# Score rests ahead of the values, and first scores in the small tiles' banks: one change to a fused attention and expert kernel

## The chip, the cores and the metric

The kernel runs on one NeuronCore of a Trainium2 chip. The metric is device microseconds (us) of one execution, by the median of several runs. The core has a matrix engine (TensorE, called PE in the profile; its weight loads are shown apart as PEld), VectorE (DVE), ScalarE (ACT), GpSimd (POOL) and SyncE (SP, which here only issues DMAs). Each takes its own queue of instructions in order, and they wait for each other through semaphores. PE writes into PSUM, which has eight banks; a tile of 128 x 448 float32 takes one.

## What is computed

The reference chains three parts. Attention over 4 batches of 12 heads (448 tokens, 64 numbers a head) with a sigmoid in place of the softmax; a gated product; and a soft mixture of 8 experts with 4 slots each:

```python
scores = scale * np.matmul(q, k.transpose(0, 1, 3, 2)) - np.log(S)
attn = 1.0 / (1.0 + np.exp(-scores))
x = np.matmul(attn, v)
...
x = (x @ w_a) * (x @ w_b) @ w_out
...
logits = x @ phi
d = softmax of logits over the tokens
slot_input = d.T @ x
h = np.maximum(slot_input[e] @ w1[e], 0.0)
slot_out[e] = h @ w2[e]
c = softmax of logits over the slots
return c @ slot_out
```

## The kernel before

**Pairs and groups.** Attention works on pairs of heads, numbered g = 0 to 23 (six pairs a batch). Keys and queries are split into a high and a low part (`kh`, `kl`, `qh`, `ql`), and a block of scores is the sum of three matmuls per head, each 64 numbers deep, the two heads side by side on the upper and the lower half of PE's rows (`emit_S`, line 230). ScalarE turns each block into weights `a` with a sigmoid (`sigmoid`, line 247, instruction at 249). The values are matmuls of `a` with `v` (`emit_PV`, line 268; lines 273, 279, 286), and their result is copied out in `emit_x` (line 303).

**Pairs from 14 on** (`GQ` = 14) are laid out otherwise than those ahead of them. Their 448 keys are cut into three blocks of 128 (first, second and third scores, c = 0, 1, 2) and a rest of 64. The rests of two neighbouring pairs, so of a group of four heads, are put together into two full blocks: `emit_S_rest` (line 252), called at the odd pair, does both pairs' rests with four matmuls of 64 x 64 (line 258). They use the whole query and a copy `kr` of the last 64 keys. It then issues, at pairs 15 and 19, the four DMAs of a later query.

**Order.** `att` (line 321) is a generator that writes the instructions in a fixed order; at each `yield` the main loop may put in a step of other work (`fill_step`: group products, logits; and operands of the next stage). A step of `att` for pair g is: split keys and queries of pair g + 1 (`emit_TK`, on VectorE: transpose, high part, low part, for keys and for queries), first scores of pair g (for pair 23 also the second ones; `first`, line 328), values of pair g - 1, second and third scores of pair g, and, at an odd pair, the rest. The main loop leaves `att` at line 1145, once the rest of pair 23 is written; the values of pair 23 come later, between the first products of the next stage (line 843).

**PSUM banks.** While attention runs, the eight banks are shared out by tags: four `sc`, two `ab`, two `ms`. A tile of a tag takes the bank that has been longest in use, and its first matmul waits until the last reader of that bank's former tile is done. `ms()` hands out the small tiles' banks: transposes (line 624, read by a copy at line 626), small transposes of the logits (line 919, read at line 920), the values of pairs 12 and 13 (line 273), the first scores of the odd pairs from 15 on, and the rests. First scores of the even pairs from 14 on, and all second and third scores, take `sc`. `emit_S` picks the tag:

```python
by_ms = c == 0 and (g % 2 if g >= GQ else g >= GT0)
sc = [ms((n, S)) if by_ms and (g >= GQ or not h) else ps_tile("ab" if ab else "sc", [n, S], 2 if ab else 4)
      for h in range(2)]
```

**After attention** come two batches' products in seven parts (line 843), the last batch's products (line 660), and the experts, whose weights stream in by DMA through a ring of buffers (lines 1229 to 1323).

Of the kernel before, what the change touches and what calls it, by code (L numbers as in the profile page):

```python
# [18 lines left out]
B, H, S, D = 4, 12, 448, 64  # L19
DM, FF, NS, NE, F = 768, 1536, 32, 8, 1024  # L20
C = 4
# [5 lines left out]
NP = H // 2  # L27
NE1, NE2 = 17, 4
ST0, ST1, PP, RAWS = 10, 39, (3, 7), (2, 3, 10, 14)
GT0 = 2 * NP + 1  # L30
GQ = 2 * NP + 2
# [9 lines left out]
def body(ctx, tc, q, k, v, w_a, w_b, w_out, phi, w1, w2, out):  # L41
# [19 lines left out]
    def ps_tile(tag, shape, bufs):  # L61
        return psp.tile(shape, F32, tag=tag, name=tag, bufs=bufs)
# [6 lines left out]
    def ms(shape=(128, S)):  # L69
        tags = banks[run["banks"]]  # L70
        tag = tags[run["ms"] % len(tags)]
        run["ms"] += 1
        return ps_tile(tag, list(shape), 4 if tag == "sc" else 2)
# [53 lines left out]
    def chunks_of(g):  # L127
        return (T, C) if g < GQ else (128, 3)
# [71 lines left out]
    def emit_TK(g):  # L200
        if g >= B * NP:
            return
        if g >= GT0:
            for nm in "kq":
                t = transposed(g, nm)
                split_heads(g, nm, t, dve.tensor_copy)
                if g >= GQ:
                    if nm == "k":
                        kr = atp.tile([128, 64], F32, tag="kr", name="kr", bufs=3)
                        act.copy(kr, t[:, 384:])  # L210
                        t = kr
                    whole[nm, g] = t
                if nm == "k" or g not in (GQ + 2, GQ + 6):
                    load_qkv(g + 3, nm)
            return
        tk = transposed(g, "k")
        if not g:
            tq = transposed(g, "q")
        split_heads(g, "k", tk, dve.tensor_copy)
        if not g:  # L220
            split_heads(g, "q", tq, act.copy)

    def emit_TQ(g):
        if g >= B * NP:
            return
        split_heads(g, "q", transposed(g, "q"), dve.tensor_copy)

    a_t = {}

    def emit_S(g, chunks):  # L230

        (kh, kl), (qh, ql) = stk[g]["k"], stk[g]["q"]
        n, _ = chunks_of(g)
        for c in chunks:
            ab = (g < NP or 2 * NP < g < GQ) and c == 2
            by_ms = c == 0 and (g % 2 if g >= GQ else g >= GT0)
            sc = [ms((n, S)) if by_ms and (g >= GQ or not h) else ps_tile("ab" if ab else "sc", [n, S], 2 if ab else 4)
                  for h in range(2)]
            cs = slice(c * n, (c + 1) * n) if g < GQ else slice(c, 384, 3)
            for i, (kx, qx) in enumerate(((kh, qh), (kl, qh), (kh, ql))):  # L240
                for h in range(2):
                    r = slice(64 * h, 64 * h + 64)
                    pe.matmul(sc[h], kx[r, cs], qx[r], start=(i == 0), stop=(i == 2))  # L243
            for h in range(2):
                sigmoid(g, h, c, sc[h], n)

    def sigmoid(g, h, c, sc, n):
        a = atp.tile([128, S], F32, tag="a", name="a", bufs=11)[:n]
        act.activation(a, sc, AF.Sigmoid, bias=nlog[:n], scale=1.0 / math.sqrt(D))  # L249
        a_t[g, h, c] = a  # L250

    def emit_S_rest(g):

        sc = [ms() for _ in range(2)]
        for d in range(2):
            for h in range(2):
                r, f = slice(64 * h, 64 * h + 64), 64 * d
                pe.matmul(sc[h][f:f + 64], whole["k", g - 1 + d][r], whole["q", g - 1 + d][r], start=True, stop=True)
        for h in range(2):
            sigmoid(g, h, 3, sc[h], 128)  # L260
        for d in range(2):
            del whole["k", g - 1 + d], whole["q", g - 1 + d]
        if g in (GQ + 1, GQ + 5):
            load_qkv(g + 4, "q")
# [3 lines left out]
    def emit_PV(g):  # L268
        if g < GQ:
            pv = pv_t[g] = ps_tile("sc", [128, S], 4) if g < 2 * NP else ms()  # L270
            for c in range(C):
                for h in range(2):
                    pe.matmul(pv[64 * h:64 * h + 64], qkv_t["v", g][:, h, c, :], a_t.pop((g, h, c)),  # L273
                              start=(c == 0), stop=(c == C - 1))
            return
        pv = pv_t[g] = ps_tile("ab", [128, S], 2)
        for c in range(3):
            for h in range(2):
                pe.matmul(pv[64 * h:64 * h + 64], qkv_t["v", g][:, h, c], a_t.pop((g, h, c)),  # L279
                          start=(c == 0), stop=False)  # L280
        if g % 2:
            a = [a_t.pop((g, h, 3)) for h in range(2)]
            for d in range(2):
                for h in range(2):
                    s = slice(64 * d, 64 * d + 64)
                    pe.matmul(pv_t[g - 1 + d][64 * h:64 * h + 64], qkv_t["v", g - 1 + d][s, h, 3], a[h][s],  # L286
                              start=False, stop=True)
# [15 lines left out]
    def emit_x(g):  # L303
        pv = pv_t.pop(g)
        qkv_t.pop(("v", g))
        b, kk = divmod(g, NP)
        if b:
            xt[g] = raw_x(b, kk)
            (dve.tensor_copy if g > GQ and g % 2 else act.copy)(xt[g], pv)
        else:  # L310
            xh = x0p.tile([128, S], F32R, tag=f"xh{kk}", name=f"xh{kk}")
            xl = x0p.tile([128, S], F32R, tag=f"xl{kk}", name=f"xl{kk}")
            act.activation(xh, pv, AF.Copy)
            dve.tensor_tensor(xl, pv, xh.bitcast(F32), op=ALU.subtract)
            xt[g] = (xh, xl)
        if g < GQ:
            load_qkv(g + 3, "v")
        if g >= GQ - 1 and g % 2:
            load_qkv(g + 4, "v")

    def att():

        emit_TK(0)
        yield 860
        for g in range(B * NP + 1):
            more = g < B * NP
            dense = g < NP or g >= 2 * NP
            first = ((0, 1) if g in (0, B * NP - 1) else (0,) if dense else ()) if more else ()
            if g:
                emit_TK(g + 1)  # L330
                if g > GQ and g % 2:
                    load_qkv(g + 3, "v")
                yield 430
            for c in first:
                emit_S(g, (c,))
                run["done"] = True
                yield 800
            if g:
                if g < NP and more:
                    emit_TQ(g + 1)  # L340
                    yield 430
                emit_PV(g - 1)
                if g <= GQ:
                    emit_x(g - 1)
                elif g % 2 == 0:
                    emit_x(g - 2)
                    emit_x(g - 1)
                yield 3200
            else:
                emit_TK(g + 1)  # L350
                yield 430
            if not more:
                return
            if not dense:
                emit_S(g, (0, 1))
                yield 1600
                emit_TQ(g + 1)
                yield 430
                emit_S(g, (2, 3))
                yield 1600  # L360
            else:
                if not g:
                    emit_TQ(g + 1)
                    yield 430
                for c in range(chunks_of(g)[1]):
                    if c not in first:
                        emit_S(g, (c,))
                        yield 800
                if g >= GQ and g % 2:
                    emit_S_rest(g)  # L370
                    yield 800

    PAIR = 860 + 4 * 800 + 3200
    att_g = att()
    att_state = [0]

# [193 lines left out]
    def fill_step():  # L570
        while fill:
            if next(fill[0], 0) is None:
                return
            fill.pop(0)
# [561 lines left out]
    for cost in att_g:  # L1136
        if then and then[0][0] in xt:
            then.pop(0)[1]()
        if not run.pop("trans", False):
            fill_step()  # L1140
        run.pop("done", None)
        if next(ops, 0) == 0:
            pu = pu or prep_u(0)
            next(pu, None)
        if (4 * NP - 1, 0, C - 1) in a_t:
            break
    run.pop("exp")()
    for _ in ops:
# [95 lines left out]
    for n in range(0, len(order1), 4):  # L1244
        _, g, x, _ = order1[n]
# [103 lines left out]
```

## Time and profile before

| | |
|---|---|
| runs | 664.79, 665.39, 662.77 us; median 664.79 |
| profiled execution | 664.73 us, of which the span of the program is 662.8 us |
| PE | busy 633.0 us, 96% of the span |
| VectorE, ScalarE, GpSimd | 380.1, 296.6 and 308.4 us |
| DMA | 154.25 MB, mean 233 GB/s |
| first scores of pair 14 | at 219.77 us |
| values of pair 23 begin | at 278.79 us |

The span runs from the first instruction to the last; the profiled execution's own time is that of the same execution as the runs are timed. In timelines a line gives the start, the time from the start of the first to the end of the last instruction merged in it, and, in brackets, how long the engine had been idle before and what ended that. An operand is named output<-inputs. `128*64` is the shape of PE's array that a matmul uses (rows by columns). Ends of matmuls are modelled, so the distance between starts is the safer reading.

### The profile page before, as it was taken

What the parts mean: (1) busy time and instruction counts of PE and PEld (TensorE: products, weight loads), DVE (VectorE), ACT (ScalarE), POOL (GpSimd) and SP (SyncE); (2) the same over time, 40 slices, a digit from 0 to 9 for tenths busy, and PEclk for the clock granted to TensorE, in tenths of its full rate; (3) what the DMA queues carried; (4) which work ended last, traced back from release to release, by engine and by line L of the source; (5) the groups of instructions that cost most, each with busy time, mean ns of one, the idle gap of its engine ahead of it and who ended that gap; (6) DMA issues with size and microseconds to landing.
All of it is one profiled execution on the core that took longest, in us unless ns stands there. A gap on an engine that the chain in (4) does not pass through costs nothing.

```text
span 662.8 us, 10904 instructions
## 1 busy us (share of the span) xinstructions
PE 633.0 (96%) x4015; PEld 449.9 (68%) x4015; DVE 380.1 (57%) x557; ACT 296.6 (45%) x534; POOL 308.4 (47%) x236
## 2 busy tenths in 40 slices
PE   6999999999999999999999999999999998997685
PEld 4557777777776555489988989888879895442121
DVE  4765797788774879588777766744324322200013
ACT  4888889889774677754423322202010002110022
POOL 0233676777644248579976575543334441000000
PEclk9999999999999999999999999999999999998798
DMA  9998999989968676501213423242999999999998
GB/s 204 280 258 221 298 305 291 314 268 300 278 166 184 112 150 143 179 1 47 96 49 103 111 89 101 69 134 80 347 372 333 384 369 344 410 415 416 409 374 303
DMA packets 145396, 154.25 MB, mean 233 GB/s; under 512 B 74336, under 2 KB 121792, under 8 KB 142272
## 3 DMA queue, kind: packets, MB, share of 16 engines
q1 hardware_dynamic: 138768, 150.01, 72.5%
q10 hardware_dynamic: 6576, 3.56, 1.9%
q8 instruction: 32, 0.52, 0.3%
q14 instruction: 20, 0.16, 0.1%
HBM read 126.36 MB, written 27.17 MB: 232 GB/s over the span
## 4 chain that ended last, share of the span: by engine, by line
PE 83%; DMA 11%; ACT 2%; DVE 2%; issue 1%; ACTq 1%; SPq 0%; DVEq 0%
PE ab L660 28%; PE sc L843 16%; DMA e<-in_moe_w 9%; PE sc L243 8%; PE ab L843 8%; PE sc L273 5%; PE ab L279 3%; PE ms L195 2%; PE ms L936 2%; PE ms L581 1%; DMA gkp<-in_moe_w 1%; PE ms L480 1%; PE ms L493 1%; PE ab L243 1%; ACT a L249 1%; PE ab L286 1%
## 5 line engine op out<-in xcount | busy, mean ns | idle before, releaser
L454 POOL TENSOR_TENSOR w<-gk,cy 128x768 int32<-128x768 int32 x36 | 66.2, 1842 | 80.1 <-DVE gk L449 35.3
L249 ACT ACTIVATE a<-sc,sums 112x448 f32<-112x448 f32 (+1 forms) x147 | 83.1, 650 | 15.8 <-PE sc L243 15.7
L660 PE MATMUL ab<-t,wh 128*128 128x448 f32 x288 | 65.1, 371 | 0.0
L660 PEld LDWEIGHTS ab<-t,wh 128*128 128x128 f32 x288 | 53.4, 188 | 6.1 <-issue 1.3
L551 POOL TENSOR_TENSOR wl<-wr,wh 128x768 fp32r<-128x768 f32 x16 | 29.5, 1841 | 49.7 <-DVE wh L550 31.9
L551 POOL TENSOR_TENSOR wl<-w,wh 128x768 fp32r<-128x768 f32 x24 | 45.0, 1878 | 10.1 <-ACT wh L550 10.1
L667 ACT COPY misc<-ab 128x448 f32<-128x448 f32 x24 | 12.7, 531 | 82.1 <-PE ab L660 75.2
L1275 PE MATMUL ab<-e,gk 128*32 128x384 f32 x240 | 34.3, 560 | 9.5 <-DMA e<-in_moe_w 9.5
L670 DVE TENSOR_TENSOR misc<-misc,ab 128x448 f32<-128x448 f32 x24 | 14.8, 616 | 43.9 <-PE ab L660 43.9
L273 PE MATMUL sc<-a,vn 112*64 112x448 f32 x192 | 38.7, 545 | 0.2 <-ACT a L249 0.2
L243 PE MATMUL sc<-qh,kh 64*112 64x448 f32 (+1 forms) x147 | 34.9, 447 | 1.0 <-ACT qh L183 0.6
L723 ACT CAST wx<-T 128x384 fp32r<-128x384 f32 x21 | 10.8, 513 | 55.7 <-DVE T L745 39.1
L660 PE MATMUL ab<-xh,wh 128*128 128x448 f32 x144 | 34.9, 377 | 0.0
L660 PE MATMUL ab<-xl,wh 128*128 128x448 f32 x144 | 34.7, 376 | 0.0
L724 POOL TENSOR_TENSOR wx<-T,wx 128x384 fp32r<-128x384 f32 x23 | 24.6, 1070 | 21.1 <-ACT wx L723 18.0
L660 PE MATMUL ab<-xh,wl 128*128 128x448 f32 x144 | 34.3, 373 | 0.0
L660 PE MATMUL ab<-t,wl 128*128 128x448 f32 x144 | 34.3, 373 | 0.0
L724 POOL TENSOR_TENSOR wx<-wr,wx 128x384 fp32r<-128x384 f32 x29 | 32.4, 1117 | 3.7 <-ACT wx L723 3.6
L1322 DVE COPY o<-sc 128x384 f32<-128x384 f32 x10 | 5.4, 554 | 48.2 <-PE sc L1301 47.0
L447 DVE TENSOR_SCALAR mf<-gk 128x768 f32<-128x768 f32 x24 | 22.7, 947 | 17.2 <-ACT gk L430 17.2
L660 PEld LDWEIGHTS ab<-xl,wh 128*128 128x128 f32 x144 | 25.9, 188 | 9.4 <-issue 7.7
L1275 PEld LDWEIGHTS ab<-e,gk 128*32 128x32 f32 x240 | 9.8, 120 | 32.8 <-DMA e<-in_moe_w 20.7
(492 smaller groups left out, 1526.6 us busy)
## 6 DMA issues: line engine op xcount, KB each, us to landing
e<-in_moe_w SPq DMA_DIRECT2D x23, 1024.0 KB, 8.5
e<-in_moe_w SPq DMA_DIRECT2D x23, 768.0 KB, 15.1
wr<-ab SPq DMA_DIRECT2D x14, 768.0 KB, 4.4
ab<-w SPq DMA_DIRECT2D x24, 384.0 KB, 6.4
gk<-gk SPq DMA_DIRECT2D x24, 224.0 KB, 4.0
e<-in_moe_w SPq DMA_DIRECT2D x14, 384.0 KB, 8.8
wr_cv<-in_moe_w_a SPq DMA_DIRECT2D x6, 768.0 KB, 7.9
wr_all<-in_moe_w_b SPq DMA_DIRECT2D x6, 768.0 KB, 6.8
```

Of the source, the lines that this page charges most:

```text
L243: pe.matmul(sc[h], kx[r, cs], qx[r], start=(i == 0), stop=(i == 2))
L249: act.activation(a, sc, AF.Sigmoid, bias=nlog[:n], scale=1.0 / math.sqrt(D))
L273: pe.matmul(pv[64 * h:64 * h + 64], qkv_t["v", g][:, h, c, :], a_t.pop((g, h, c)), start=(c == 0), stop=(c == C - 1))
L279: pe.matmul(pv[64 * h:64 * h + 64], qkv_t["v", g][:, h, c], a_t.pop((g, h, c)), start=(c == 0), stop=False)
L447: dve.tensor_scalar(mf, m, LOW, HIGH, op0=ALU.max, op1=ALU.min)
L454: pool.tensor_tensor(thirds(w), m.bitcast(I32), thirds(cy_t.pop(x)), op=ALU.add)
L551: pool.tensor_tensor(wl, t, wh.bitcast(F32), op=ALU.subtract)
L660: pe.matmul(t, w[:, kk * 128:(kk + 1) * 128], xt[b * NP + kk][xi], start=(s == 0 and kk == 0), stop=(s == 2 and kk == KD - 1))
L670: dve.tensor_tensor(g, g, t, op=ALU.mult)
L724: pool.tensor_tensor(w[:, 1], t, w[:, 0].bitcast(F32), op=ALU.subtract)
L843: pe.matmul(t, w[:, wi, k * 128:(k + 1) * 128], xs[ORDER[m], k][xi], start=(s == 0 and k == 0), stop=(s == 2 and k == 2))
L1275: pe.matmul(sps[h][32 * j:32 * j + 32], hT[:, 2 * x + i, 2 * j + g], ring[order2[n + j]][0][:, i, c0:c0 + w], start=(g == 0 and x == 0 and ...
```

## The change

First scores of every pair from 13 on are now handed to `ms` (for pairs from 14 on both heads' tiles), the rests take `sc` banks, and the rest of a group is written in the odd pair's step right after its first scores and ahead of the even pair's values. Since the rest of pair 23 is now written earlier, the main loop's end looks for its third scores.

```diff
--- before.py
+++ after.py
@@ -233,7 +233,7 @@
         n, _ = chunks_of(g)
         for c in chunks:
             ab = (g < NP or 2 * NP < g < GQ) and c == 2
-            by_ms = c == 0 and (g % 2 if g >= GQ else g >= GT0)
+            by_ms = c == 0 and g >= GT0
             sc = [ms((n, S)) if by_ms and (g >= GQ or not h) else ps_tile("ab" if ab else "sc", [n, S], 2 if ab else 4)
                   for h in range(2)]
             cs = slice(c * n, (c + 1) * n) if g < GQ else slice(c, 384, 3)
@@ -251,7 +251,7 @@
 
     def emit_S_rest(g):
 
-        sc = [ms() for _ in range(2)]
+        sc = [ps_tile("sc", [128, S], 4) for _ in range(2)]
         for d in range(2):
             for h in range(2):
                 r, f = slice(64 * h, 64 * h + 64), 64 * d
@@ -334,6 +334,9 @@
             for c in first:
                 emit_S(g, (c,))
                 run["done"] = True
+                yield 800
+            if more and g > GQ and g % 2:
+                emit_S_rest(g)
                 yield 800
             if g:
                 if g < NP and more:
@@ -366,9 +369,6 @@
                     if c not in first:
                         emit_S(g, (c,))
                         yield 800
-                if g >= GQ and g % 2:
-                    emit_S_rest(g)
-                    yield 800
 
     PAIR = 860 + 4 * 800 + 3200
     att_g = att()
@@ -1142,7 +1142,7 @@
         if next(ops, 0) == 0:
             pu = pu or prep_u(0)
             next(pu, None)
-        if (4 * NP - 1, 0, C - 1) in a_t:
+        if (4 * NP - 1, 0, C - 2) in a_t:
             break
     run.pop("exp")()
     for _ in ops:
```

How this moves the instructions, at the places that the prediction speaks of. On PE at pair 14 (`ident` is the identity that a transpose multiplies by, `misc` what is transposed, `a` and `vn` weights and values of pair 13, `ls_d` the logits):

```order
 L243 MATMUL sc<-ql,kh 112x448 x2
 L624 MATMUL ms<-ident,misc 128x128 x4
-L243 MATMUL sc<-qh,kh 128x448 x2
-L243 MATMUL sc<-qh,kl 128x448 x2
-L243 MATMUL sc<-ql,kh 128x448 x2
+L243 MATMUL ms<-qh,kh 128x448 x2
+L243 MATMUL ms<-qh,kl 128x448 x2
+L243 MATMUL ms<-ql,kh 128x448 x2
 L273 MATMUL ms<-a,vn 64x448 x8
 L919 MATMUL ms<-ident,ls_d 112x32 x4
```

The order is the same; pair 14's first scores, between a transpose and the values of pair 13, have gone from `sc` to `ms` banks, as all their neighbours have.

On VectorE at the same place, in the changed kernel; nothing moved here against the kernel before (`gk_94` takes the transposes of line 624, `kn` and `qn` are keys and queries of pair 15):

```order
L626 COPY gk_94<-ms 128x512 [waits PE_49] x2
L191 STREAM_TRANSPOSE kn<-kn 128x448 [waits DMAHW7_49,DMAHW6_49,DMAHW0_49]
L183 CAST kh<-kn 128x448 [waits DVE_49,PE_49]
L184 TENSOR_TENSOR kl<-kn,kh 128x448 [waits DVE_49]
L191 STREAM_TRANSPOSE qn<-qn 128x448 [waits DMAHW6_49,DMAHW7_49,DMAHW1_49,DMAHW0_49]
L183 CAST qh<-qn 128x448 [waits DVE_49]
L184 TENSOR_TENSOR ql<-qn,qh 128x448 [waits DVE_49]
L626 COPY gk_94<-ms 128x512 [waits PE_49]
L920 COPY ls_d<-ms 112x128 [waits PE_49]
```

The third copy, of the transpose that stands right ahead of pair 14's first scores on PE, comes behind the six instructions that split pair 15. The last row reads the small transpose that PE makes after pair 13's values.

On PE in the first group of four heads, after pair 15's first scores:

```order
 L243 MATMUL ms<-qh,kl 128x448 x2
 L243 MATMUL ms<-ql,kh 128x448 x2
+L258 MATMUL sc<-qn,kr 64x448 x4
 L279 MATMUL ab<-a,vn 64x448 x6
 L243 MATMUL sc<-qh,kh 128x448 x2
```

and one step further on, after pair 15's third scores:

```order
 L243 MATMUL sc<-qh,kl 128x448 x2
 L243 MATMUL sc<-ql,kh 128x448 x2
-L258 MATMUL ms<-qn,kr 64x448 x4
-L243 MATMUL sc<-qh,kh 128x448 x2
-L243 MATMUL sc<-qh,kl 128x448 x2
-L243 MATMUL sc<-ql,kh 128x448 x2
+L243 MATMUL ms<-qh,kh 128x448 x2
+L243 MATMUL ms<-qh,kl 128x448 x2
+L243 MATMUL ms<-ql,kh 128x448 x2
 L279 MATMUL ab<-a,vn 64x448 x6
```

The rest has moved from behind the third scores of pair 15 to ahead of pair 14's values (line 279), and from `ms` to `sc`; pair 16's first scores now follow on pair 15's third scores, in `ms`. The three groups behind it are moved alike. In the last one the rest stood between pair 23's third scores and the first product (line 843) and now stands ahead of pair 22's values. The order on SP and on GpSimd is the same as before.

## Rows read from the trace of the kernel before

**Rows 1.** The page's chain that ended last: shares of the span by engine.
```profile
PE 83%; DMA 11%; ACT 2%; DVE 2%; issue 1%; ACTq 1%; SPq 0%; DVEq 0%
```

**Rows 2.** Timeline of PE around pair 14: start us, us, engine line op out<-in xcount.
```profile
219.18 0.66 PE L624 MATMUL ms<-ident,misc 128*128 128x128 f32 x4
...
219.77 0.54 PE L243 MATMUL sc<-qh,kh 64*128 64x448 f32 x2
...
220.65 3.23 PE L273 MATMUL ms<-a,vn 112*64 112x448 f32 x16
...
223.83 0.40 PE L919 MATMUL ms<-ident,ls_d 32*112 32x32 f32 x4
...
224.16 0.54 PE L243 MATMUL sc<-qh,kh 64*128 64x448 f32 x2
```

**Rows 3.** Timeline of VectorE (DVE) over the same stretch.
```profile
218.21 1.27 DVE L626 COPY gk<-ms 128x512 f32<-128x512 f32 x2
...
219.41 0.63 DVE L191 STREAM_TRANSPOSE kn<-kn 128x448 f32<-128x448 f32 x1
...
223.09 0.68 DVE L626 COPY gk<-ms 128x512 f32<-128x512 f32 x1
...
224.27 0.29 DVE L920 COPY ls_d<-ms 112x128 f32<-112x128 f32 x1 [0.49 <-PE ms L919]
```

**Rows 4.** The list of waits, 222 to 283 us: us in total, times, longest.
```profile
PEld ms L919 <- DVE gk L626: 0.7, 1, 0.7
```

**Rows 5.** Timeline of ScalarE (ACT): pair 14's first and second scores.
```profile
220.81 1.16 ACT L249 ACTIVATE a<-sc,sums 128x448 f32<-128x448 f32 x2 [0.18 <-PE sc L243]
...
225.21 0.64 ACT L249 ACTIVATE a<-sc,sums 128x448 f32<-128x448 f32 x1 [0.73 <-PE sc L243]
...
225.21 1.16 ACT L249 ACTIVATE a<-sc,sums 128x448 f32<-128x448 f32 x2 [0.73 <-PE sc L243]
```

**Rows 6.** Timeline of PE around the rest of pairs 14 and 15.
```profile
226.27 2.48 PE L279 MATMUL ab<-a,vn 128*64 128x448 f32 x12
...
229.88 0.37 PE L243 MATMUL sc<-ql,kh 64*128 64x448 f32 x2
...
230.17 0.98 PE L258 MATMUL ms<-qn,kr 64*64 64x448 f32 x8
...
231.09 0.54 PE L243 MATMUL sc<-qh,kh 64*128 64x448 f32 x2
...
231.47 0.36 PE L243 MATMUL sc<-qh,kl 64*128 64x448 f32 x2
...
231.67 0.37 PE L243 MATMUL sc<-ql,kh 64*128 64x448 f32 x2
```

**Rows 7.** Stretches near the end; third from last number: granted clock (first: PE busy).
```profile
604.07:607.48 3.41, 1.30 (x8) 0.24 (x10) 0.00 (x0) 0.00 (x0) 0.00 (x0) 1.00 1.03 422
...
607.48:610.89 3.41, 3.41 (x24) 1.13 (x26) 0.00 (x0) 0.00 (x0) 0.00 (x0) 0.50 1.01 414
...
617.72:621.13 3.41, 1.35 (x4) 0.28 (x4) 0.00 (x0) 0.00 (x0) 0.00 (x0) 1.00 1.02 416
...
621.13:624.55 3.42, 2.53 (x17) 0.71 (x20) 0.00 (x0) 0.00 (x0) 0.00 (x0) 0.50 1.02 417
...
624.55:627.96 3.41, 3.31 (x22) 0.72 (x14) 0.00 (x0) 0.00 (x0) 0.00 (x0) 0.50 1.01 402
```

**Rows 8.** Timeline of PE in the fourth group of four heads.
```profile
265.65 0.54 PE L243 MATMUL sc<-ql,kh 64*128 64x448 f32 x2 [0.48 <-DVE ql L184]
```

**Rows 9.** Timeline of ACT, then PE, at pairs 22 and 23.
```profile
270.49 1.16 ACT L249 ACTIVATE a<-sc,sums 128x448 f32<-128x448 f32 x2 [0.39 <-PE sc L243]
...
271.46 0.77 PE L243 MATMUL sc<-qh,kh 64*128 64x448 f32 x2
...
272.57 0.97 PE L279 MATMUL ab<-a,vn 128*64 128x448 f32 x4
```

**Rows 10.** The chain of waits in order of time: start us, us, what.
```profile
573.54 10.98 DMA e<-in_moe_w
```

## The prediction

> **What bounds the kernel now.** I read the chain of waits first. Work of TensorE (PE) is 83% of it, DMA 11% [rows 1]; the DMA part is one late stretch, in which PE waits for expert weights [rows 10]. So a microsecond lost or won on PE at 220 us arrives at the end, unless something else is late at the same place. I then read PE's order of time around pair 14, the first pair of the new layout. There PE goes without a gap from a transpose (219.18) to the pair's first scores (219.77), to pair 13's values (220.65) and on to a small transpose (223.83) [rows 2]. The reader is to see that nothing waits there, and then what VectorE does meanwhile: two copies out of `ms` banks end at 219.48, six instructions that split pair 15 start at 219.41, and the third copy comes only at 223.09, ending at 223.77 [rows 3]. That copy is of the transpose that PE made at 219.18. The list of waits names it as what the small transpose at 223.83 waited for [rows 4]; it costs nothing today, because pair 13's values fill the time.
>
> **Part 1: first scores of the even pairs take the `ms` banks.** There are two `ms` banks. At pair 14 the order of use is: transpose, transpose, first scores of head 0, first scores of head 1, values of pair 13, small transpose. Each use takes the bank of the use two places before. Until now the two scores stood in `sc` banks, the values took the first transpose's bank (free at 219.48) and the small transpose the second's (free at 223.77). Now head 0 takes the first (free), and head 1 takes the bank that VectorE empties at 223.77.
> - The wait. PE reaches head 1 at 219.77. The bank is free at 223.77, and the small transpose started 0.06 later [rows 2, 3]. So head 1 starts at 223.83: 4.06 us lost. All of PE's later work is queued behind it, and VectorE's next instruction (the copy of the small transpose, 224.27) waits for PE in turn, so it does not run ahead meanwhile.
> - The values' wait. They now need head 0's bank, so they wait for its sigmoid. The scores take 0.88 us (219.77 to 220.65) [rows 2], so PE would be ready at 224.71. The sigmoid starts 1.04 after the scores began (220.81) and lasts 0.64 [rows 2, 5]: 223.83 + 1.04 + 0.64 + 0.05 = 225.56, up to 0.85 late; head 0's first matmul is already done, which takes up to 0.2 off. I take 0.7. Together 4.06 + 0.7 = 4.76, say **4.8 us**.
> - The other even pairs (16, 18, 20, 22): the bank was last used by the pair before, a whole pair earlier, and its sigmoid is long done. Cost 0.
>
> **Part 2: TensorE's clock.** The stall leaves PE idle from about 220.1 to 223.8 and again for 0.7. In this trace the granted clock fell to half (1.2 instead of 2.4 GHz) behind the stretch 604.07 to 607.48, in which PE was busy 1.30 of 3.41 us, and again behind one with 1.35; it stayed at half for 3.41 us once and for 6.83 the other time [rows 7]. The stall has less work in it than either, so I expect a fall. What half clock costs is half of the busy time in it: 3.41 / 2 = 1.7, or (2.53 + 3.31) / 2 = 2.9 [rows 7]. The values' wait lies inside the slow stretch, as waits did in the second case, but nothing waits after it, as in the first; so I take the middle, **2.3 us**. Lower end 0 (no fall), upper end 2.9.
>
> **Part 3: the rests move in front of the values.** The rest's four matmuls per group of four heads (five groups: pairs 15, 17, 19, 21, 23) are as many as before. What changes is their neighbours. Score steps are 0.20 apart (231.47 to 231.67); from the last score to the rest it is 0.29, and the first score step behind it takes 0.38 (231.09 to 231.47) [rows 6]. These extras, 0.09 + 0.18 = 0.27, go away, since the rest now stands beside the values and the step from scores to values exists already. Counting the last group, where the rest stood before a product and not before a score, alike, the whole gain is at most 5 x 0.27 = 1.35 us.
> How far this holds was weighed against the Trainium skill, TensorEngine Tiling (Array Packing), Tiling Modes, which says that each change of tiling mode drains the array. By it rest (64x64) to values (128x64) is still a change, so of the two changes at the old place one is saved and the sum stays 1.35; a reader who took two neighbours of one data type for free would count another 0.18 per group.
> Against the gain stands a new wait: the rest's second bank is now the one of the even pair's second scores, whose sigmoids in the first group end 1.16 after 225.21, at 226.37 [rows 5]; PE is there at 226.27, where the values start now [rows 6]. With 0.05 for the signal that is 0.15 per group, leaving 0.12. In the third and fourth groups even this is lost, because PE waits for VectorE's low part of a query (265.65) [rows 8], a chain that started from a score of the third group and does not get shorter. So 2 x 0.12, and half of one for the last group with its other neighbour, make **0.3 us** gained; ends: 1.35 gained (no wait for the sigmoid) and 0.65 lost (rival C).
> The rest issues 4 query loads at pairs 15 and 19. Nothing else is issued on SP between the old and the new place, so SP's order stays, and GpSimd's (POOL) too; 0. ScalarE does the same sigmoids in another order; 0.
>
> **Sum.** 664.73 (the profiled execution, 0.06 under the median of the three runs) + 4.8 + 2.3 - 0.3 = **671.5 us**, about 1.0% slower.
>
> **The rivals.**
> - A: the same wait, but the clock does not fall. 664.73 + 4.8 - 0.3 = 669.2. For it: PE works without a gap before the stall. Against it: two falls in this trace behind stretches with 1.3 us of work in them [rows 7].
> - B, not slower: head 1 does not wait, because the third copy is done early. It decides at one point: the copy must be over by 219.8. Then only part 3 counts, 664.4, at best 663.4. Against it: the copy stands behind six instructions that VectorE has to finish, and the small transpose was seen waiting for it [rows 3, 4]. The Trainium skill (TensorE: Matmul & The Clock Gate, Architectural detail) says that VectorE is strictly first in, first out; the rows agree, the copy is the last of the seven to start.
> - C, more than the forecast: the rest's wait costs more than itself. At 271.46 scores stand in front of a bank that a sigmoid frees at 270.49 + 1.16 = 271.65, and the block takes 1.11 to 272.57 [rows 9] where three steps of 0.20 and one start of 0.09 make 0.70. A wait of 0.2 cost 0.4. Then each group loses 0.40 - 0.27 = 0.13, all five 0.65, in place of 0.3 won: 664.73 + 4.8 + 2.3 + 0.65 = 672.5; with the long clock fall (2.9) 673.1.
>
> **How the numbers follow.** Forecast (wait and clock fall) 0.70, A 0.17, B 0.08, C 0.05. The range reaches from A with the whole gain, 664.73 + 4.8 - 1.35 = 668.2, to C with the long fall and the 0.85, rounded up to 673.4; only B lies outside. A measurement of this kernel tells 0.5% (3.3 us) from no change. The forecast, A and C lie above that, except A with a measurement at the edge of the runs' spread (0.01): slower 0.91. B is within it for 0.06, with that 0.01 of A: same 0.07. The other 0.02 of B are faster, where the runs' own spread adds to its best end.
>
> **What would show it.** In the changed profile: a gap on PE of about 4 us right behind the transpose near 219, its releaser VectorE's copy at line 626; a second, shorter one before pair 13's values, released by a sigmoid; granted clock 0.50 for 3 to 7 us from about 222 to 230; scores of pair 14's second chunk starting near 229 to 231 instead of 224.16. Each later group of four heads should take 0.1 to 0.3 us less than now, with the rest starting up to 0.15 behind the score in front of it. The forecast is wrong if PE shows no gap at 220, if the clock stays full there, or if a later group gains or loses more than 0.3.

## The result and the profile after

| | before | after |
|---|---|---|
| median of the runs | 664.79 us (662.77 to 665.82, 5 runs) | 672.22 us (671.40 to 672.84, 5 runs) |
| profiled execution, span | 664.73, 662.8 us | 672.45, 670.7 us |
| values of pair 23 begin, after pair 14's first scores | 59.02 us | 67.04 us |

The ratio is 1.0112, 95% interval 1.0091 to 1.0133: the change makes the kernel slower by 7.4 us. The last row of the table puts 8.02 us between pair 14's first scores and pair 23's values, and the span is 7.9 longer, so the whole loss arises inside the stretch that the change touches.

The page of the changed kernel: its span, the busy time of PE, and the shares of the chain that ended last, which answer to [rows 1].

```profile
span 670.7 us, 10884 instructions
...
PE 637.0 (95%) x4015; PEld 452.0 (67%) x4015; DVE 381.0 (57%) x557; ACT 296.7 (44%) x534; POOL 308.8 (46%) x236
...
PE 83%; DMA 11%; ACT 2%; DVE 2%; issue 1%; ACTq 0%; SPq 0%; DVEq 0%
```

The shares read as they did. PE is busy for 4 us more with the same instructions, and idle for another 4: that split (a gap, and slower work) is the story of the result, but the page alone does not say where.

PE's timeline around pair 14, against [rows 2]:

```profile
219.07 0.66 PE L624 MATMUL ms<-ident,misc 128*128 128x128 f32 x4
219.66 0.53 PE L243 MATMUL ms<-qh,kh 64*128 64x448 f32 x1
223.70 0.61 PE L243 MATMUL ms<-qh,kh 64*128 64x448 f32 x1 [3.51 <-DVE gk L626]
...
225.48 5.87 PE L273 MATMUL ms<-a,vn 112*64 112x448 f32 x16 [0.42 <-ACT a L249]
231.28 0.41 PE L919 MATMUL ms<-ident,ls_d 32*112 32x32 f32 x4
231.62 0.54 PE L243 MATMUL sc<-qh,kh 64*128 64x448 f32 x2
```

Head 0 starts at 219.66, head 1 alone at 223.70, and the bracket names who let it go: VectorE's copy at line 626. The values wait a second time, for a sigmoid. Then sixteen matmuls of values, which took 3.18 from their start to the small transpose (220.65 to 223.83 in [rows 2]), take 5.80 (225.48 to 231.28).

VectorE over the same stretch, against [rows 3]:

```profile
222.97 0.68 DVE L626 COPY gk<-ms 128x512 f32<-128x512 f32 x1
...
231.72 0.29 DVE L920 COPY ls_d<-ms 112x128 f32<-112x128 f32 x1 [8.07 <-PE ms L919]
```

The copy stands where it stood, relative to PE; it ends at 223.65, and head 1 starts 0.05 later. VectorE then has nothing for 8.07 us, since its next instruction waits for a transpose behind the late values.

Windows of the same kernel; the numbers behind the window are its length, PE's busy time, and (third from last) the granted clock.

```profile
219.00:222.00 3.00, 1.19 (x7) 0.66 (x5) 2.83 (x6) 1.29 (x3) 1.49 (x2) 1.00 0.50 109
222.00:225.00 3.00, 1.30 (x5) 0.74 (x5) 1.61 (x3) 0.21 (x1) 0.00 (x0) 0.84 0.58 93
225.00:228.00 3.00, 2.58 (x9) 1.00 (x10) 0.00 (x0) 0.95 (x2) 0.00 (x0) 0.50 0.68 138
228.00:231.00 3.00, 3.00 (x10) 0.72 (x8) 0.00 (x0) 0.00 (x0) 0.00 (x0) 0.53 0.28 75
231.00:234.00 3.00, 3.00 (x27) 2.44 (x27) 1.56 (x4) 1.87 (x4) 0.00 (x0) 1.00 0.13 19
```

Behind the gap the clock is granted at half (1.2 instead of 2.4 GHz). The means 0.84, 0.50 and 0.53 of three windows make 0.96 + 3.00 + 2.82 = 6.8 us at half, the longer of the two stretches of [rows 7]. It begins near 224.04 (225.00 - 0.96), so it holds the end of the scores and almost all of the values.

Last, the chain in order of time, for the late transfer that [rows 10] show at 573.54:

```profile
581.46 11.02 DMA e<-in_moe_w
```

It is 7.92 later, as the values of pair 23 are (278.79 before, 286.70 after: 7.91). So nothing between 287 and 581 us gave any of the loss back.

### The profile page after: what moved, and what is told of

The parts are those of the page before. It is cut to its first block, busy times and chain, and to the rows that moved or that the text cites. A ratio compares the mean times of both kernels' runs of the same rounds, so it can differ in the third digit from the quotient of the medians.

```text
span 670.7 us, 10884 instructions
## 1 busy us (share of the span) xinstructions
PE 637.0 (95%) x4015; PEld 452.0 (67%) x4015; DVE 381.0 (57%) x557; ACT 296.7 (44%) x534; POOL 308.8 (46%) x236
## 4 chain that ended last, share of the span: by engine, by line
PE 83%; DMA 11%; ACT 2%; DVE 2%; issue 1%; ACTq 0%; SPq 0%; DVEq 0%
PE ab L660 27%; PE sc L843 16%; DMA e<-in_moe_w 8%; PE ab L843 7%; PE sc L243 7%; PE sc L273 5%; PE ab L279 3%; PE ms L195 2%; PE ms L936 2%; PE ms L581 1%; DMA gkp<-in_moe_w 1%; PE ms L480 1%; PE ms L243 1%; PE ms L493 1%; PE ms L273 1%
## 5 line engine op out<-in xcount | busy, mean ns | idle before, releaser
L243 PE MATMUL sc<-qh,kh 64*112 64x448 f32 (+1 forms) x137 | 32.1, 438 | 1.0 <-ACT qh L183 0.6
```

## The experiments

The theory was that of the prediction: pair 14's head 1 takes a bank that VectorE empties late; the gap lets the clock fall; what the moved rests do is small beside it. The rivals: the gap costs only itself (A), the loss is not that wait (B), or the rests lose by their new banks (C). Runs with a ratio were timed beside the kernel before on the same chip (664.10 us, 14 runs, for the first four; 664.19, 17 runs, for the fifth). The ratios, with their 95% intervals, differ a little from the quotients of the medians.

**1. The change without pair 14's part.** Pair 14 keeps its `sc` banks; everything else of the change stays.

```diff
-            by_ms = c == 0 and g >= GT0
+            by_ms = c == 0 and g >= GT0 and g != GQ
```

> The change, but the first scores of pair 14 alone stay in sc banks; all else is as in the change. Theory (the bank that VectorE empties late, and the clock behind it): the two gaps on PE at 220 us go, pair 14's second scores start again near 224.1 instead of 231.6, the clock stays full there, and the rests still cost a little (groups of 11.2 us): 665.2 us, between 664.5 and 666. Rival (the moved rests are what costs, the gap is met anyway by what follows): 670 to 672.

Measured: 664.64 us, ratio 1.0003 (0.9990 to 1.0016). PE's timeline of this run, pair 14 and the first rest:

```profile
219.85 0.54 PE L243 MATMUL sc<-qh,kh 64*128 64x448 f32 x2
...
220.73 3.23 PE L273 MATMUL ms<-a,vn 112*64 112x448 f32 x16
...
226.36 1.34 PE L258 MATMUL sc<-qn,kr 64*64 64x448 f32 x8
227.63 2.48 PE L279 MATMUL ab<-a,vn 128*64 128x448 f32 x12
```

The gap, the fall and the loss are gone with that one condition: the granted clock is 1.00 in every window from 219 to 231 us. What is left of the change gains nothing: the values of pair 23 begin 59.50 us behind pair 14's first scores, 0.48 later than before, which is less than these runs can tell from nothing. The rest takes 1.27 from its start to the values, where it took 0.91 in [rows 6] (230.17 to 231.09, read between starts).

**2. Pair 14's part alone**, in the kernel before.

```diff
-            by_ms = c == 0 and (g % 2 if g >= GQ else g >= GT0)
+            by_ms = c == 0 and (g % 2 or g == GQ if g >= GQ else g >= GT0)
```

> The kernel before with one thing of the change: the first scores of pair 14, and of no other even pair, go to ms banks; the rests stay where they were, in ms. Theory: the whole loss comes back, a gap of 4.0 us and one of 0.4 to 0.8 on PE, then 3.4 to 6.8 us at half clock: 7.4 us more than before, 672.2, between 669 and 673. Rival (the moved rests are what costs): 665, as before.

Measured: 671.09 us, ratio 1.0115 (1.0096 to 1.0134). PE's timeline of this run:

```profile
218.85 0.53 PE L243 MATMUL ms<-qh,kh 64*128 64x448 f32 x1
222.91 0.74 PE L243 MATMUL ms<-qh,kh 64*128 64x448 f32 x1 [3.52 <-DVE gk L626]
...
230.71 0.54 PE L243 MATMUL sc<-qh,kh 64*128 64x448 f32 x2
```

The second chunk of pair 14 starts 11.86 behind the first, where it was 4.39 before (219.77 to 224.16, [rows 2]): 7.47 lost at this one place. Runs 1 and 2 are each the other's complement, and the loss goes with pair 14: from its first scores to pair 23's values it is 7.45 longer than before in run 2 (66.47), and 0.48 in run 1.

**3. The same change, with the late copy on ScalarE.** The last of the four copies out of the transposes' banks (the third of those in VectorE's order above) is given to ScalarE, which is free by then; it no longer stands behind the six instructions on VectorE.

```diff
-        gr, lg = group(0, 2, (dve.tensor_copy,) * 4), LG(0)
+        gr, lg = group(0, 2, (dve.tensor_copy,) * 3 + (act.copy,)), LG(0)
```

> The change, but the third copy that head 1's bank waits for is done by ScalarE in place of VectorE. ScalarE ends its last sigmoid and a small copy at about 220.5 us. Theory (it is VectorE's six instructions ahead of the copy, not the bank as such): the copy ends near 221.1, PE's first gap shrinks from 4.0 to about 1.5 us, the second stays at 0.4 to 0.8; if the clock stays full, 664.8 + 2.2 + 0.4 = 667.4 us, if it falls all the same about 669.5. Rival (two ms banks are too few whoever empties them): gap of 4 us, 672.

Measured: 667.19 us, ratio 1.0053 (1.0036 to 1.0070). PE's timeline of this run:

```profile
219.03 0.53 PE L243 MATMUL ms<-qh,kh 64*128 64x448 f32 x1
220.43 0.54 PE L243 MATMUL ms<-qh,kh 64*128 64x448 f32 x1 [0.87 <-ACT gk L626]
...
221.97 3.23 PE L273 MATMUL ms<-a,vn 112*64 112x448 f32 x16 [0.59 <-ACT a L249]
```

And ScalarE's:

```profile
219.78 0.60 ACT L626 COPY gk<-ms 128x512 f32<-128x512 f32 x1
```

And its windows, the granted clock third from last:

```profile
219.00:222.00 3.00, 1.54 (x9) 0.92 (x8) 2.79 (x6) 2.10 (x6) 0.87 (x1) 1.00 0.31 82
222.00:225.00 3.00, 3.00 (x16) 1.02 (x16) 0.43 (x1) 0.44 (x1) 0.00 (x0) 1.00 0.67 108
```

Now head 1 starts 0.05 behind the end of that copy, 1.40 behind head 0. Moving the copy moved the wait: it is the copy's place in VectorE's queue, not its length, that makes 4 us. The clock stays full, in the same program with a gap of 0.87 in place of 3.51. The two waits come to 221.97 - 219.03 - 0.88 = 2.06 us: 1.40 for the bank and, from head 1 to the values, 221.97 - 220.43 - 0.88 = 0.66 for the sigmoid. In this trace pair 23's values begin 2.47 later than before, counted from pair 14's first scores, which is these waits and some 0.4 of the rests. The median is 3.1 higher, but the runs reach from 665.85 to 668.72, and the profiled one is the lowest of them.

**4. The wait kept, PE kept busy in it.** Eighteen matmuls that repeat head 0's first product, into its own bank, stand ahead of pair 14's first scores; the scores start the bank afresh, so no value changes.

```diff
+            for _ in range(18 if (g, c) == (GQ, 0) else 0):
+                pe.matmul(sc[0], kh[:64, cs], qh[:64], start=True, stop=True)
```

> The change, with 18 more matmuls of pair 14's first head put ahead of its first scores, into the same bank (the real scores write over them), so that PE works for about 3.4 us of the 4.0 that it waits. Theory (the clock's fall is a loss of its own): the wait for VectorE still ends near 223.7, pair 13's values start near 225.2, but the granted clock stays at full and the values take 3.2 us instead of 5.8: 672.2 - 2.6 = 669.6 us. Rival (the wait costs all of it, or the clock falls for another reason): 672 or more.

Measured: 669.77 us, ratio 1.0086 (1.0071 to 1.0101). PE's timeline of this run (lines are two higher), head 1's first weight load, and one window:

```profile
219.76 4.01 PE L241 MATMUL ms<-qh,kh 64*128 64x448 f32 x18
223.61 0.73 PE L245 MATMUL ms<-qh,kh 64*128 64x448 f32 x2
...
225.34 3.23 PE L275 MATMUL ms<-a,vn 112*64 112x448 f32 x16 [0.59 <-ACT a L251]
...
228.83 0.54 PE L245 MATMUL sc<-qh,kh 64*128 64x448 f32 x2
```

```profile
223.81 0.25 PEld L245 LDWEIGHTS ms<-qh,kh 64*128 64x128 f32 x1 [0.15 <-DVE gk L628]
```

```profile
225.00:228.00 3.00, 2.66 (x14) 1.06 (x16) 0.00 (x0) 0.81 (x2) 0.00 (x0) 1.00 0.69 135
```

The wait is as long as ever: head 1 starts at 223.81, 4.05 behind 219.76, and only head 0, whose bank nobody else holds, starts at 223.61. The clock stays full. So the fall is not tied to the place or to what else runs there: here it follows from PE having nothing to do. This is rival A's case: 669.8 us, where it had 669.2. The second wait can be read here without the clock in it: 225.34 - 223.81 - 0.88 = 0.65, as in run 3. So can the price of the clock: second scores start 9.07 behind the start at 219.76, in the change 11.96 behind 219.66, and the waits are the same, so half clock cost 2.89.

**5. The rest behind the even pair's values**, in `ms` banks as before, with run 1's condition for pair 14. This was a try for a version that beats both.

```diff
-            if more and g > GQ and g % 2:
-                emit_S_rest(g)
-                yield 800
...
+                if more and g > GQ and g % 2:
+                    emit_S_rest(g)
+                    yield 800
```

(The second place is right behind the line that writes the even pair's results; `emit_S_rest` has `sc = [ms() for _ in range(2)]` again.)

> First scores in ms for the pairs from 15 on, pair 14's in sc; the rest of a group is written right behind the even pair's values (not ahead of them) and stays in ms. Theory (in the change the rest takes 1.25 us in place of 0.91 because it waits for the sigmoid of the even pair's second scores, not because rest and values do not go together): behind the values no bank is late, the rest takes 0.91 again, the 0.27 of the two saved steps is kept, groups of 10.85 to 10.9 us where VectorE is not late, the fourth still held by VectorE: 0.5 to 1.1 us less than before, 663.0 to 663.9. Rival (a rest beside values costs 1.25 wherever it stands): groups of 11.2, 664.5.

Measured: 664.13 us, ratio 1.0001 (0.9984 to 1.0017), so no gain that can be measured. PE's timeline of this run, first and last rest:

```profile
228.05 1.15 PE L258 MATMUL ms<-qn,kr 64*64 64x448 f32 x8
229.13 0.54 PE L243 MATMUL sc<-qh,kh 64*128 64x448 f32 x2
...
274.21 0.98 PE L258 MATMUL ms<-qn,kr 64*64 64x448 f32 x8
275.12 0.54 PE L243 MATMUL sc<-qh,kh 64*128 64x448 f32 x2
```

Neither side came out clean: the rest takes 1.08 to 1.11 in four groups, neither 0.91 nor 1.25. There are two `ms` banks and a rest takes both, so it waits for the odd pair's first sigmoids. The last rest, which comes later behind them, takes 0.91. Three groups are 11.06 to 11.07 long, where the kernel before has 11.12, and from pair 14's first scores to pair 23's values it is 58.89 us in place of 59.02.

**6. Two extra matmuls ahead of the odd pairs' first scores**, on top of run 1, which bring PE 0.20 later to the rest.

```diff
+            for h in range(2 if c == 0 and g > GQ and g % 2 else 0):
+                r = slice(64 * h, 64 * h + 64)
+                pe.matmul(sc[h], kh[r, cs], qh[r], start=True, stop=True)
```

> As the kernel with pair 14 in sc, and ahead of the first scores of the pairs 15, 17, 19, 21 and 23 their first two matmuls once more, into the same banks (the real scores write over them): 0.20 us more work on PE per group, so that PE comes to the rest 0.20 later than now, 0.05 behind the sigmoid that frees the rest's second bank. Theory (the rest's 1.25 us are 0.91, a wait of 0.15 and a restart of 0.19 that any wait brings): the rest takes 0.91 again, and a group is 0.34 - 0.20 = 0.14 shorter with more work in it: 11.05 us in place of 11.19. Rival (rest beside values costs 1.25 by itself): the rest stays at 1.25, groups of 11.4.

Measured, one run: 664.05 us beside 663.80. PE's timeline of this run, first rest:

```profile
225.68 1.11 PE L261 MATMUL sc<-qn,kr 64*64 64x448 f32 x8
226.71 2.48 PE L282 MATMUL ab<-a,vn 128*64 128x448 f32 x12
```

The rest takes 1.03, so 0.2 more work in front of it cost nothing: the first three groups stay 11.18 to 11.20 long, as in run 1. That part of the rest's 1.25 is the wait for the bank. But 0.12 over the 0.91 was left, though the sigmoids had ended 0.1 before PE came.

**7. Eight extra matmuls** in the same place, to tell whether those 0.12 belong to the bank or to the new neighbours.

```diff
-            for h in range(2 if c == 0 and g > GQ and g % 2 else 0):
+            for h in (0, 1) * (4 if c == 0 and g > GQ and g % 2 else 0):
```

> The run before this one left 0.13 us open: with two extra matmuls (0.20 us) ahead of the odd pairs' first scores the rest took 1.03 in front of the values instead of 1.25, but not the 0.91 that it takes at its old place, although the bank was free 0.1 before PE came. Here eight extra matmuls instead of two (four score steps, 0.82 us), so the bank is free some 0.7 before. Theory W (all of it is the bank: the rest's weights are loaded some 0.2 ahead of a matmul where nothing holds them, and the bank held them back): the weight load starts before the last score step ends and the rest takes 0.87 to 0.95. Theory S (0.13 belongs to the place between scores and values, with or without a wait): the rest stays at 1.02 to 1.06. Each group of four heads is then longer than the 11.19 of the change by 0.82 - 0.34 = 0.48 by W (11.67), by 0.82 - 0.21 = 0.61 by S (11.80). Whole time: 664.05 + 5 x (0.82 - 0.20) less 0.1 per group by W.

Measured, one run: 665.46 us beside 664.16. PE's timeline of this run, two group starts and first rest:

```profile
222.84 0.54 PE L246 MATMUL sc<-qh,kh 64*128 64x448 f32 x2
...
225.77 0.98 PE L261 MATMUL sc<-qn,kr 64*64 64x448 f32 x8
226.68 2.48 PE L282 MATMUL ab<-a,vn 128*64 128x448 f32 x12
...
234.51 0.54 PE L246 MATMUL sc<-qh,kh 64*128 64x448 f32 x2
```

Theory W: the rest takes 0.91, a group 11.67. All 0.34 were the bank. The whole time came out below the number expected (the values of pair 23 lie 60.86 behind pair 14's first scores, 1.33 more than in run 6, not 2.6): in the fourth group the extra work also covered the wait for VectorE, and in the last that for a sigmoid ahead of the third scores, which the expectation had not counted.

## Why the prediction was right, and which terms were off

Forecast 671.5 us, measured 672.22. The mechanism and its place were right, and so were both waits. The clock's term was too small, and the term of the rests had the wrong sign. Counted between pair 14's first scores and pair 23's values:

| term | predicted | in the trace after | how read |
|---|---|---|---|
| wait for the bank | 4.06 | 4.04 | 219.66 to 223.70 |
| values' wait for the sigmoid | 0.7 | 0.66 | run 3, without the clock in it |
| half clock | 2.3 | 2.87 | second scores 7.57 later, less 4.04 and 0.66 |
| rests moved | -0.3 | +0.45 | 0.06 + 0.07 + 0.07 - 0.12 + 0.37, below |
| sum | 6.8 | 8.02 | 67.04 - 59.02 |

By its terms the forecast was 1.2 us short. That it missed the median by only 0.7 is in part luck: the medians lie 7.4 apart, the two profiled executions 7.7.

- **The wait.** Head 0 free, head 1 behind the third copy, 0.05 for the signal: as the rows gave it. Runs 1 and 2 show that the whole loss but for the rests starts there, run 3 that its length is set by the copy's place in the queue. Rival B, for which the copy had to be over by 219.8, fell with the row of 3.51.
- **The values' wait.** The working gave up to 0.85 and took off 0.15, because head 0's first matmul is done early. That was right: in run 3, where it is early too, the wait is 0.66, and in run 4 0.65.
- **The clock.** The prediction took the middle between a short stretch at half (1.7) and a long one (2.9). It was the long one, 6.8 us, so 2.9 was the better end, and second scores start at 231.62, behind the 229 to 231 that were named; run 4, with the same waits at full clock, gives 2.89. Values at half take 5.80 - 3.18 = 2.62 longer, and the end of the scores lies in the stretch too. Rival A fell with the windows; run 4 is the kernel that it spoke of.
- **The rests moved.** This step had the wrong sign. Groups are measured from one start of second scores to the next: 224.16, 235.28, 246.40, 257.52 and 269.44 before, 231.62, 242.80, 253.99, 265.18 and 276.98 after. Three groups are 0.06 to 0.07 longer, the fourth is 0.12 shorter, and the last, to pair 23's values, 0.37 longer. The prediction's signs had said 0.1 to 0.3 less for each, and that it is wrong if one gains or loses more than 0.3: on this part it was.

PE's timeline of the changed kernel at the first rest, at the fourth group's wait for VectorE (0.48 in [rows 8]), and at the last rest, with ScalarE's sigmoids behind it:

```profile
233.72 1.32 PE L258 MATMUL sc<-qn,kr 64*64 64x448 f32 x8
234.97 2.48 PE L279 MATMUL ab<-a,vn 128*64 128x448 f32 x12
...
273.20 0.53 PE L243 MATMUL ms<-ql,kh 64*128 64x448 f32 x2 [0.26 <-DVE ql L184]
...
280.12 1.34 PE L258 MATMUL sc<-qn,kr 64*64 64x448 f32 x8
281.39 2.48 PE L279 MATMUL ab<-a,vn 128*64 128x448 f32 x12
...
284.68 0.88 PE L843 MATMUL sc<-A11h,wx 128*128 128x448 f32 x3
285.39 0.77 PE L843 MATMUL sc<-A11l,wx 128*128 128x448 f32 x3
```

```profile
232.66 2.21 ACT L249 ACTIVATE a<-sc,sums 128x448 f32<-128x448 f32 x4 [0.73 <-PE sc L243]
...
278.03 2.21 ACT L249 ACTIVATE a<-sc,sums 128x448 f32<-128x448 f32 x4 [0.41 <-PE sc L243]
```

The saving itself is real. In run 7, where the bank is free, a group less the extra work is 11.67 - 0.82 = 10.85, the predicted 0.27 under 11.12. The Trainium skill (TensorEngine Tiling (Array Packing), Tiling Modes) says that a change of tiling mode drains the array. By it rest (64x64) to values (128x64) still pays, and the trace agrees: 0.27 went, and not the 0.45 (0.27 + 0.18) of the prediction's reader who takes that change for free. What failed is the wait set against it: the prediction priced it at the time until the sigmoid's end plus 0.05, 0.15 in all, and it costs 1.25 - 0.91 = 0.34. That is rival C's mechanism, a wait that costs more than itself; C took 0.40 from a similar block. So 0.34 - 0.27 = 0.07 is lost per group instead of 0.12 won. On this part it was C, given 0.05, that came true, with 0.45 lost in all where it had 0.65, and its sum of 672.5 lies nearer to 672.22 than the forecast's.

The prediction had groups three and four gain nothing, because of VectorE: the third has no such wait in either trace and lost 0.07 like the first two, and the fourth did gain 0.12, its wait for VectorE having shrunk from 0.48 to 0.26. And the last group gained nothing from its new order, against the half of a group's gain that was counted: a product behind scores pays its own start (284.68 to 285.39, 0.71), the same 0.71 that it paid behind the rest (276.77 to 277.48 before, the lines below), while the rest costs 1.27 where it cost 0.92 (275.85 to 276.77).

```profile
275.85 0.98 PE L258 MATMUL ms<-qn,kr 64*64 64x448 f32 x8
276.77 0.87 PE L843 MATMUL sc<-A11h,wx 128*128 128x448 f32 x3
277.48 0.77 PE L843 MATMUL sc<-A11l,wx 128*128 128x448 f32 x3
```

The upper end of the range, 673.4, is not the sum that it is said to be: the terms named there give 673.2. Nothing hangs on it.

## What to carry to other kernels

When a tile moves to another ring of banks, write down the ring's order of use, and for each new user find the instruction that empties the bank and where it stands in its engine's queue: here one of the moved tiles met a copy that had six instructions ahead of it, and that was nearly the whole result. A wait that nobody felt because other work lay over it (the third copy, before) becomes a price as soon as a tile in front of that work needs the same bank. On PE the price has a second part, the clock behind the gap, which run 4 took away at the unchanged wait; and a gain of a quarter of a microsecond from a better neighbour is lost if the new place reaches its bank a tenth too early.

## What was not expected of the hardware

A bank has to be free some time before PE reaches it, if the block behind it is not to get longer. Seven of the places, with PE's arrival at the block, the end of the last sigmoid that frees its banks, and by how much the block was longer than without a wait (0.91 for a rest, 0.70 for scores):

| place | PE there | sigmoid ends | end less arrival | longer by |
|---|---|---|---|---|
| after, first rest | 233.72 | 233.82 | 0.10 | 0.34 |
| after, last rest | 280.12 | 280.24 | 0.12 | 0.36 |
| run 5, first rest | 228.05 | 227.98 | -0.07 | 0.17 |
| run 6, first rest | 225.68 | 225.57 | -0.11 | 0.12 |
| run 7, last rest | 273.07 | 272.79 | -0.28 | 0.01 |
| run 7, first rest | 225.77 | 225.05 | -0.72 | 0 |
| before, third scores [rows 9] | 271.46 | 271.65 | 0.19 | 0.41 |

(Sigmoids: start of the pair's row plus 1.16 for two, in run 5 1.19, or 2.21 for four. The 0.01 is within the reading.) In the five rows that are clearly longer, it is longer by the fourth column plus 0.22 to 0.24. A bank free 0.11 ahead was too late, one free 0.28 ahead was not. The 0.05 that a PE already idle needs after the release (head 1 at pair 14, in the changed kernel and in run 3) is only a part of that. PE's weight loads of the rest show where the rest of it lies; first in the changed kernel, then in run 7:

```profile
233.72 0.55 PEld L258 LDWEIGHTS sc<-qn,kr 64*64 64x64 f32 x8 [0.24 <-issue]
```

```profile
225.77 0.21 PEld L261 LDWEIGHTS sc<-qn,kr 64*64 64x64 f32 x8 [0.25 <-ACT a L252]
```

The eight loads of a rest stand within 0.21 us when the bank is free, and are drawn out to 0.55 when it is not, 0.34 more, as the block. It may be that the two heads, whose steps otherwise start together, fall out of step; that was not tried, and the rule is read from such places alone. (The second to fourth rests of the changed kernel read alike: 0.33 to 0.36 longer at 0.09 to 0.10.)
